# Order of a fused attention, gated convolution and feed-forward kernel: first loads and last block's steps rewritten

## The chip, the cores and the metric

One core of a Trainium2 chip (trn2) runs the kernel. The metric is the device time of one execution in microseconds; the median of the runs counts. The page and the trace come from one profiled execution. Engines: PE is TensorE, DVE VectorE, ACT ScalarE, POOL GpSimd, and SP is SyncE, whose queue issues all 360 DMA instructions of this kernel.

## What is computed

8 sequences of 576 tokens, 8 heads of 64 channels, all in float32. Attention runs in chunks of 64 tokens; its output, 512 channels, is gated by a causal convolution of five taps, and a normalized feed-forward part of 2048 hidden channels is added to it.

```python
scores = scale * np.matmul(q_c, k_c.transpose(0, 1, 2, 4, 3))      # per chunk of 64
attn = np.exp(scores - np.max(scores, axis=-1, keepdims=True))
attn = attn / (np.sum(attn, axis=-1, keepdims=True) + 1e-09)
x = np.matmul(attn, v_c)                                           # then (B, S, 512)
gate = 1.0 / (1.0 + np.exp(-sum(conv_w[k] * xp[:, k:k + S, :])))   # 5 taps, causal
x = gate * (x @ w_val) @ w_out
xn = (x - mu) / np.sqrt(var + 1e-06) * g_ln
out = x + np.maximum(xn @ w_ch1, 0.0) @ w_ch2
```

## The kernel before

The 4608 tokens are 18 units `u` of 256 tokens for the attention and 9 blocks `j` of 512 tokens for the gated part. Two units make a block. Products that need more than one pass of precision are split into a high and a low part, and three products are summed.

The steps of a unit: `sc(u)` (PE, 64 small matmuls of q and k), `mx` and `sub` (DVE, row maximum and difference), `exp` (ACT), `total` and `norm` (DVE, row sum, reciprocal and product), `turn` (PE, eight transposes), `turned` (ACT, copy to the tile pT), `pv` (PE, 64 small matmuls with v), `full`, `high`, `less`, `low` (ACT, ACT, PE, ACT: the result in full, its high part, the difference, its low part; tiles xf, xh, xl).

The steps of a block: `tap` and `taps` (ACT, DVE: the convolution), `sigm` (ACT), `val(j,f)` (PE, 12 matmuls), `gate`, `gate_high`, `gate_low` (DVE, ACT, DVE: product with the gate, its two parts gh and gl), `proj(j,t)` (PE, 12 matmuls over f = 0 to 3), `put(j,t)` (ACT copy and store). In block 0 two of the four channel groups run their convolution on PE: `conv_pe(f)`, ten matmuls, with `diag` and `sigm_pe` on ACT. `projp(j,t,f)` is a quarter of `proj`, three matmuls.

Weights arrive as pairs of 32-bit words and are unpacked: `w_copy` (ACT), `w_bits` (DVE, two instructions on the tile da), `w_high` (ACT), `w_low` (GpSimd). The prefix `ff_` marks the same steps for the first eight loads of the feed-forward weights, `ff_load(k)`, `ff_copy(k)` and so on. Block 0 of the feed-forward part is normalized beside block 8 of the gated part: `load_y0` (read of the stored block into yt0, 1 MB), `stats0`, `scale_a` to `scale_c`, `apply0`, `turn0`, `turned0`, `xn_high`, `xn_low`. Then come `ff1` and `ff2` of block 0, and the other eight blocks in four pairs.

What sets the order: up to the end of block 8's gated part, PE, DVE, ACT and SP follow a list of steps written out by hand, each engine in the order of that list (`tc.manual_schedule`). The first period (attention of units 0 to 5, block 0) is such a list; `period(j)` for j = 1 to 6 is a function that repeats; then blocks 7 and 8 are a list again. Behind it, only PE is ordered by hand.

The loads of the first period in this kernel: `load_qk(0)` to `load_qk(2)`, `load_v(0)` to `load_v(2)` and the four of `w_val` are issued ahead of the list (lines 759 to 770). `sc(u)` then issues `load_qk(u+2)`, `pv(u)` issues `load_v(u+3)`, and the step `load_o` issues the four loads of `w_out` together. A load of q and k is 1 MB, one of v or of a weight 0.5 MB. A load waits in SP's queue until its buffer is free (q and k have two buffers, v three), and what is queued behind it on SP waits too.

Of the kernel before, what the change touches and what calls it, by code (L numbers as in the profile page):

```python
# [10 lines left out]
U32 = mybir.dt.uint32  # L11
# [8 lines left out]
def tile_chunk_attention_gated_mlp(ctx: ExitStack, tc: tile.TileContext, qk, v, w_val, conv_w, w_out, g_ln, w1, w2, out):  # L20
# [143 lines left out]
    def sc(u):  # L164
        t = qkr.pop(u)
        kt, qt = t[:, 0], t[:, 1]
        ps = tsc[u] = ps_s.tile([P, 2, NG, CH], F32, tag="sc", name="sc")
        for g in range(NG):
            n, hp = divmod(g, NP)
            for c in range(2):  # L170
                cs = slice(n * P + c * CH, n * P + (c + 1) * CH)
                for par in range(2):
                    r0 = CH * par
                    nc.tensor.matmul(  # L174
                        out=ps[CH * c:CH * c + CH, par, g, :], lhsT=qt[r0:r0 + CH, hp, cs], rhs=kt[r0:r0 + CH, hp, cs],
                        start=True, stop=True,
                    )
        if 0 < u < NU - 2:
            load_qk(u + 2)

    def mx(u):
# [68 lines left out]
    def pv(u):  # L250
        t, va = tpT.pop(u), vr.pop(u)
        x = tx[u] = ps_x.tile([P, 2, NP // 2, UN], F32, tag="x", name="x")
        for i in range(NP // 2):
            for c in range(NC):
                n, cs = c // 2, slice(c % 2 * CH, (c % 2 + 1) * CH)
                for f in range(2):
                    for r in range(2):
                        r0, o0 = CH * r, CH * f
                        nc.tensor.matmul(  # L259
                            out=x[o0:o0 + CH, r, i, c * CH:(c + 1) * CH],  # L260
                            lhsT=va[r0:r0 + CH, c, 2 * i + f, :],
                            rhs=t[r0:r0 + CH, n * NP + 2 * i + f, cs],
                            start=(i == 0 and c == 0), stop=False, skip_group_check=True,
                        )
        if u + 3 < NU:
            load_v(u + 3)

    def part(t, u):
# [491 lines left out]
    cwu = stg.tile([KC * CT, P, 2], U32, tag="raw", name="cwu")  # L760
    nc.sync.dma_start(out=cwu.rearrange("r p w -> r (p w)"), in_=conv_w.rearrange("k (c p) w -> (k c) (p w)", p=P))
    nc.sync.dma_start(out=gr, in_=g_ln.rearrange("(c p) -> c p", p=P))
    load_w(w_val, "v", 0, 0, 1)
    load_qk(1)
    load_v(0)
    load_w(w_val, "v", 0, 1, 2)
    load_qk(2)
    load_v(1)
    load_w(w_val, "v", 0, 2, 4)
    load_v(2)  # L770

    s_0 = ExitStack()
    xn0, yt0, ps_t = None, None, None

# [122 lines left out]
        hs, ls = wv[nm + "s"]  # L897
        eng.tensor_tensor(out=ls[c], in0=fa.pop((nm, c)), in1=hs[c], op=ALU.subtract)

    def load_o():  # L900
        load_w(w_out, "o", CT)

    def diag(f):
        for i in range(KC):
# [79 lines left out]
        cnv(sigm, 3)  # L984

    with tc.manual_schedule(engines={mybir.EngineType.PE, mybir.EngineType.DVE, mybir.EngineType.Activation, mybir.EngineType.SP}):
        cwr_copy()
        sc(0)
        w_copy('v',0)
        cwr_bits()  # L990
        mx(0)
        sub(0)
        cw_turn()
        w_bits('v',0)
        exp(0)
        sc(1)
        w_copy('v',1)
        cw_copy()
        total(0)
        w_high('v',0)  # L1000
        mx(1)
        diag(0)
        sub(1)
        norm(0)
        sc(2)
        exp(1)
        w_copy('v',2)
        turn(0)
        mx(2)
        sub(2)  # L1010
        turned(0)
        exp(2)
        pv(0)
        w_low('v',0,nc.gpsimd)
        total(1)
        norm(1)
        turn(1,True)
        full(0)
        high(0)
        less(0)  # L1020
        total(2)
        turned(1)
        sc(3)
        low(0)
        norm(2)
        w_copy('v',3)
        mx(3)
        sub(3)
        pv(1)
        full(1)  # L1030
        load_o()
        turn(2,True)
        sc(4)
        w_bits('v',1)
        w_bits('v',3)
        high(1)
        w_high('v',1)
        w_low('v',1,nc.gpsimd)
        w_bits('v',2)
        mx(4)  # L1040
        diag(1)
        tap(0,3)
        less(1)
        sub(4)
        low(1)
        taps(0,3)
        turned(2)
        w_high('v',2)
        exp(3)
        w_copy('o',0)  # L1050
        conv_pe(0)
        w_bits('o',0)
        w_high('v',3)
        sc(5)
        total(3)
        exp(4)
        mx(5)
        pv(2)
        w_high('o',0)
        full(2)  # L1060
        high(2)
        norm(3)
        w_low('v',2,nc.gpsimd)
        conv_pe(1)
        w_copy('o',1)
        w_low('v',3,nc.gpsimd)
        less(2)
        val(0,0)
        tap(0,2)
        low(2)  # L1070
        w_copy('o',2)
        turn(3)
        taps(0,2)
        sigm_pe(0)
        sigm(0,3)
        w_bits('o',1)
        gate(0,0)
        total(4)
        w_low('o',0,nc.gpsimd)
        turned(3)  # L1080
        val(0,1)
        sigm_pe(1)
        pv(3)
        w_copy('o',3)
        val(0,2)
        w_bits('o',2)
        w_high('o',1)
        gate_high(0,0)
        sub(5)
        w_low('o',1,nc.gpsimd)  # L1090
        high(3)
        full(3)
        w_bits('o',3)
        norm(4)
        w_high('o',2)
        less(3)
        sigm(0,2)
        val(0,3)
        gate(0,1)
        gate_low(0,0)  # L1100
        low(3)
        gate(0,2)
        w_low('o',2,nc.gpsimd)
        turn(4)
        gate_high(0,1)
        w_high('o',3)
        gate_high(0,2)
        turned(4)
        gate_low(0,1)
        gate(0,3)  # L1110
        gate_low(0,2)
        gate_high(0,3)
        tap(1,2)
        pv(4)
        exp(5)
        tap(1,3)
        tap(1,0)
        w_low('o',3,nc.gpsimd)
        gate_low(0,3)
        full(4)  # L1120
        taps(1,2)
        taps(1,3)
        taps(1,0,1,2)
        proj(0,0)
        sigm(1,3)
        taps(1,0,2)
        proj(0,1)
        proj(0,2)
        proj(0,3)
        tap(1,1)  # L1130
        high(4)
        put(0,0)
        sigm(1,2)
        sigm(1,0)
        put(0,1)
        taps(1,1)
        sigm(1,1)
        put(0,2)
        less(4)
        low(4)  # L1140
        put(0,3)
        for j in range(1, NB - 2):
            period(j)
        norm(17)
        val(7,0)
        gate(7,0)
        val(7,1)
        ff_load(0)
        gate_high(7,0)
        gate(7,1)  # L1150
        val(7,2)
        ff_copy(0)
        ff_load(1)
        gate_high(7,1)
        gate_low(7,0)
        ff_bits(0)
        ff_load(2)
        gate(7,2)
        ff_copy(1)
        ff_high(0)  # L1160
        gate_low(7,1)
        ff_bits(1)
        turn(17)
        ff_low(0)
        gate_high(7,2)
        turned(17)
        gate_low(7,2)
        ff_copy(2)
        val(7,3)
        projp(7,0,0)  # L1170
        gate(7,3)
        pv(17)
        gate_high(7,3)
        projp(7,0,2)
        projp(7,0,1)
        full(17)
        ff_bits(2)
        projp(7,1,0)
        gate_low(7,3)
        tap(8,3)  # L1180
        tap(8,2)
        tap(8,0)
        projp(7,1,3)
        taps(8,3)
        ff_load(3)
        tap(8,1)
        projp(7,1,2)
        taps(8,2)
        projp(7,2,0)
        projp(7,2,1)  # L1190
        high(17)
        projp(7,0,3)
        projp(7,1,1)
        projp(7,3,0)
        taps(8,0,1,2)
        ff_high(1)
        ff_high(2)
        taps(8,1)
        projp(7,3,2)
        taps(8,0,2)  # L1200
        ff_low(2)
        projp(7,2,3)
        put(7,0)
        put(7,1)
        ff_low(1)
        ff_copy(3)
        projp(7,2,2)
        projp(7,3,3)
        projp(7,3,1)
        less(17)  # L1210
        sigm(8,2)
        sigm(8,3)
        put(7,2)
        put(7,3)
        low(17)
        prep()
        val(8,0)
        stats0(3)
        stats0(2)
        ff_load(4)  # L1220
        stats0(1)
        sigm(8,0)
        stats0(0)
        ff_copy(4)
        scale_a()
        sigm(8,1)
        val(8,1)
        gate(8,0)
        scale_b()
        val(8,2)  # L1230
        val(8,3)
        gate_high(8,0)
        gate(8,1)
        scale_c()
        gate_low(8,0)
        gate_high(8,1)
        apply0(2)
        apply0(0)
        apply0(1)
        gate_low(8,1)  # L1240
        gate(8,2)
        projp(8,0,0)
        turn0(0)
        gate(8,3)
        projp(8,1,0)
        gate_high(8,2)
        gate_low(8,2)
        turn0(1)
        apply0(3)
        gate_high(8,3)  # L1250
        turned0(0)
        gate_low(8,3)
        projp(8,0,1)
        projp(8,0,2)
        projp(8,1,1)
        projp(8,0,3)
        turned0(1)
        projp(8,1,3)
        ff_bits(3)
        ff_load(5)  # L1260
        turn0(2)
        xn_high(0)
        ff_bits(4)
        turn0(3)
        put(8,0)
        turned0(2)
        projp(8,1,2)
        projp(8,2,0)
        put(8,1)
        projp(8,2,2)  # L1270
        ff_copy(5)
        load_y0()
        projp(8,2,3)
        ff_load(6)
        projp(8,3,0)
        turned0(3)
        xn_high(2)
        xn_low(0)
        ff_bits(5)
        projp(8,2,1)  # L1280
        projp(8,3,1)
        ff_load(7)
# [135 lines left out]
```

## Time and profile before

| | us |
|---|---|
| runs of the kernel | 1071.51, 1072.88, 1073.88; median 1072.88 |
| profiled execution | 1072.09 |
| its span in the profile | 1070.3 |
| PE busy | 1041.0 (97%) |
| VectorE busy | 676.0 (63%) |
| ScalarE busy | 495.2 (46%) |
| GpSimd busy | 47.9 (4%) |
| moved by DMA | 155.26 MB |

All stretches below are microseconds from the start of the span. Busy time of an engine counts its instructions, without waits. The granted clock of PE (PEclk) is a share of its full 2.4 GHz, so 0.50 is its lower level of 1.2 GHz. "issue" as the end of a wait means that the trace shows nothing that the engine waited for.

### The profile page before, as it was taken

How to read it: one execution, taken by the hardware profiler on the slowest of the kernel's cores; microseconds unless marked ns; L12 is line 12 of the kernel's file. 1: busy time of each engine (PE TensorE's matmuls, PEld its weight loads, DVE VectorE, ACT ScalarE, POOL GpSimd, SP SyncE). 2: the span in 40 equal slices, each digit the busy share in tenths (PEclk: the TensorE clock that was granted, in tenths of full speed). 3: DMA queues.
4: the chain of work that ended last, by engine and by line, in shares of the span. 5: the costliest groups of instructions: out<-in, count | busy, mean ns of one | idle time of the engine just before them, and what ended most of it. 6: DMA issues, size and time to landing. Idle time of an engine off the chain costs nothing.

```text
span 1070.3 us, 16857 instructions
## 1 busy us (share of the span) xinstructions
PE 1041.0 (97%) x6778; PEld 855.3 (80%) x6778; DVE 676.0 (63%) x1112; ACT 495.2 (46%) x872; POOL 47.9 (4%) x74
## 2 busy tenths in 40 slices
PE   4899999999999999999999999999999999999998
PEld 4578888888778887888888888888888888888886
DVE  6899999998858896665465454258344438333434
ACT  4687766677767864444332234333233423222211
POOL 0210000000000003222100000000000000000000
PEclk9999999999999999999999999999999999999999
DMA  9614344413379836334427234325432324522202
GB/s 354 237 61 161 136 150 149 151 67 109 128 239 304 299 138 230 140 135 147 150 97 239 96 99 137 102 95 189 146 118 99 99 88 145 190 81 97 99 21 78
DMA packets 58580, 155.26 MB, mean 145 GB/s; under 512 B 5742, under 2 KB 13958, under 8 KB 56198
## 3 DMA queue, kind: packets, MB, share of 16 engines
q1 hardware_dynamic: 58502, 154.19, 41.6%
q8 instruction: 53, 0.87, 0.3%
q14 instruction: 25, 0.20, 0.1%
HBM read 116.41 MB, written 37.75 MB: 144 GB/s over the span
## 4 chain that ended last, share of the span: by engine, by line
PE 88%; DMA 5%; DVE 3%; ACT 2%; issue 1%; SPq 0%; ACTq 0%
PE psf L631 16%; PE acc L631 16%; PE x L663 16%; PE zy L663 12%; PE psv L346 8%; PE pso L346 7%; DMA raw<-in_moe_w_ch 3%; PE sc L174 2%; PE x L259 2%; PE acc L512 2%; PE pst L224 1%; DMA qkr<-in_qk 1%; PE pst L469 1%; PE pso L404 1%; PE psh L346 1%
## 5 line engine op out<-in xcount | busy, mean ns | idle before, releaser
L692 DVE TENSOR_TENSOR c<-x,c 128x512 f32<-128x512 f32 x96 | 66.2, 690 | 230.9 <-ACT c L687 183.2
L631 PE MATMUL psf<-w,h 128*128 128x512 f32 x768 | 187.6, 389 | 0.0
L631 PE MATMUL acc<-w,h 128*128 128x512 f32 x768 | 184.3, 389 | 0.0
L631 PEld LDWEIGHTS psf<-w,h 128*128 128x128 f32 x768 | 144.1, 188 | 30.3 <-DVE yt L636 0.4
L631 PEld LDWEIGHTS acc<-w,h 128*128 128x128 f32 x768 | 144.2, 188 | 29.9
L687 ACT ACTIVATE c<-zy 128x512 f32<-128x512 f32 x96 | 58.1, 606 | 203.3 <-PE zy L663 203.3
L663 PE MATMUL x<-t,wc 128*128 128x512 f32 x576 | 146.8, 390 | 0.8 <-DVE c L692 0.8
L663 PEld LDWEIGHTS x<-t,wc 128*128 128x128 f32 x576 | 107.7, 188 | 24.7 <-DVE c L692 2.1
L315 DVE SCALAR_TENSOR_TENSOR cg<-xf,cw,cg 128x516 f32<-128x516 f32 (+1 forms) x136 | 102.0, 766 | 4.4 <-ACT cg L307 1.0
L677 ACT ACTIVATE h<-c 128x512 fp32r<-128x512 f32 x96 | 60.5, 631 | 91.7 <-DVE c L692 46.9
L636 DVE TENSOR_TENSOR yt<-psf,yt 128x512 f32<-128x512 f32 x128 | 88.1, 689 | 21.0 <-PE psf L631 20.9
L663 PE MATMUL zy<-b,wc 128*128 128x512 f32 x384 | 98.6, 392 | 0.0
L663 PEld LDWEIGHTS zy<-b,wc 128*128 128x128 f32 x384 | 71.2, 188 | 14.2
L678 DVE SCALAR_TENSOR_TENSOR h<-c,h 128x512 fp32r<-128x512 f32 x96 | 69.0, 720 | 20.1 <-ACT h L677 18.6
L677 ACT ACTIVATE h<-x 128x512 fp32r<-128x512 f32 x32 | 19.1, 596 | 96.1 <-PE x L663 96.1
L346 PE MATMUL psv<-xh,vh 128*128 128x512 f32 x144 | 58.3, 405 | 1.2 <-ACT xl L301 1.2
L346 PE MATMUL psv<-xl,vh 128*128 128x512 f32 x144 | 56.2, 391 | 0.0
L346 PE MATMUL psv<-xh,vl 128*128 128x512 f32 x144 | 56.2, 391 | 0.0
L346 PE MATMUL psh<-xn,w 128*128 128x512 f32 x192 | 47.7, 398 | 2.1 <-DVE hl L497 2.1
L663 PE MATMUL x<-b,wc 128*128 128x512 f32 x192 | 48.9, 390 | 0.1
L663 PE MATMUL zy<-t,wc 128*128 128x512 f32 x192 | 48.7, 389 | 0.0
L346 PEld LDWEIGHTS psh<-xn,w 128*128 128x128 f32 x192 | 36.6, 191 | 10.7 <-DVE hl L497 2.5
(123 smaller groups left out, 1524.7 us busy)
## 6 DMA issues: line engine op xcount, KB each, us to landing
wc<-wc SPq DMA_DIRECT2D x112, 512.0 KB, 3.2
qkr<-in_qk SPq DMA_DIRECT2D x18, 1024.0 KB, 6.7
raw<-in_moe_w_ch SPq DMA_DIRECT2D x32, 512.0 KB, 5.6
vr<-in_v SPq DMA_DIRECT2D x18, 512.0 KB, 4.2
yd<-y SPq DMA_DIRECT2D x36, 256.0 KB, 2.2
out<-yt SPq DMA_DIRECT2D x36, 256.0 KB, 3.8
yr<-yd SPq DMA_DIRECT2D x32, 256.0 KB, 3.4
yt<-yd SPq DMA_DIRECT2D x32, 256.0 KB, 5.4
```

Of the source, the lines that this page charges most:

```text
L174: nc.tensor.matmul(out=ps[CH * c:CH * c + CH, par, g, :], lhsT=qt[r0:r0 + CH, hp, cs], rhs=kt[r0:r0 + CH, hp, cs], start=True, stop=True,)
L259: nc.tensor.matmul(out=x[o0:o0 + CH, r, i, c * CH:(c + 1) * CH], lhsT=va[r0:r0 + CH, c, 2 * i + f, :], rhs=t[r0:r0 + CH, n * NP + 2 * i + ...
L315: last_tap[j] = nc.vector.scalar_tensor_tensor(out=o, in0=xf[j][:, f, i:i + n], scalar=cw[:, i * CT + f:i * CT + f + 1], in1=o, op0=ALU.mu ...
L346: nc.tensor.matmul(out=ps, lhsT=lt, rhs=rh, start=(i == 0), stop=(i == n - 1))
L512: nc.tensor.matmul(out=acc[t], lhsT=lt, rhs=rh, start=(f == 0 and i == 0), stop=(f == NF - 1 and i == 2))
L631: nc.tensor.matmul(out=ps, lhsT=lt, rhs=rh, start=(g == 0 and k == 0 and (first or half)), stop=(g == 1 and k == 2 and (last or half)),)
L636: nc.vector.tensor_tensor(out=yt[i], in0=ps, in1=yt[i], op=ALU.add)
L663: nc.tensor.matmul(out=ps, lhsT=lt, rhs=rh, start=(start and c == 0 and i == 0), stop=(c == 1 and i == 2), skip_group_check=True)
L677: last_act = nc.scalar.activation(out=t[:, 0, :], in_=src, func=ACTF.Relu)
L678: last_relu = nc.vector.scalar_tensor_tensor(out=t[:, 1, :], in0=src, scalar=0.0, in1=t[:, 0, :], op0=ALU.max, op1=ALU.subtract)
L687: nc.scalar.activation(out=t, in_=zy, func=ACTF.Copy)
L692: nc.vector.tensor_tensor(out=t, in0=x, in1=t, op=ALU.add)
```

## The change

The operations, their number and their sizes are the same in both kernels, on each engine; the low parts of the attention weights (`w_low`) run on GpSimd in both. What changes is order.

1. The loads of the first period become steps of the list, each at a place of its own, `load_o` is cut into four, and a bound keeps `sc` and `pv` from issuing these loads themselves.
2. The list of the first period has another order.
3. The list of blocks 7 and 8 has another order. `load_y0` is issued twice in both kernels, in `prep()` and near the end of block 8; the second of these moves.

```diff
+    AHEAD = 5
-        if 0 < u < NU - 2:
+        if AHEAD < u < NU - 2:
             load_qk(u + 2)
-        if u + 3 < NU:
+        if AHEAD - 1 < u < NU - 3:
             load_v(u + 3)
-    load_qk(0)
...
-    load_w(w_val, "v", 0, 2, 4)
-    load_v(2)
-    def load_o():
-        load_w(w_out, "o", CT)
+    def load_wv(c):
+        load_w(w_val, "v", 0, c, c + 1)
+
+    def load_wo(c):
+        load_w(w_out, "o", CT, c, c + 1)
     with tc.manual_schedule(engines={mybir.EngineType.PE, mybir.EngineType.DVE, mybir.EngineType.Activation, mybir.EngineType.SP}):
+        load_qk(0)
+        load_cw()
+        sc(0)
         cwr_copy()
-        sc(0)
...
```

On PE, the first steps of the first period before, from sc(1) on (rows of L174 are sc, L224 turn, L259 pv, L295 less, L336 conv_pe):

```order
L174 MATMUL sc_227<-qkr_161 64x64 x32
L174 MATMUL sc_291<-qkr_167 64x64 x32
L224 MATMUL pst_329<-ident_140,pr_289 128x128 x8
L259 MATMUL x_345<-pT_341,vr_163 64x64 x32
L224 MATMUL pst_386<-ident_140,pr_384 128x128 x4
L224 MATMUL pst_387<-ident_140,pr_384 128x128 x4
L295 MATMUL x_345<-xh_398,neg_142 128x512 x2
L174 MATMUL sc_409<-qkr_260 64x64 x32
L259 MATMUL x_453<-pT_406,vr_169 64x64 x32
```

The same steps now (lines are one higher):

```order
L175 MATMUL sc_225<-qkr_206 64x64 x32
L225 MATMUL pst_263<-ident_140,pr_220 128x128 x8
L260 MATMUL x_297<-pT_294,vr_260 64x64 x32
L175 MATMUL sc_330<-qkr_272 64x64 x32
L296 MATMUL x_297<-xh_375,neg_142 128x512 x2
L225 MATMUL pst_388<-ident_140,pr_371 128x128 x4
L225 MATMUL pst_389<-ident_140,pr_371 128x128 x4
L260 MATMUL x_408<-pT_400,vr_378 64x64 x32
L175 MATMUL sc_443<-qkr_441 64x64 x32
```

sc(2) stood ahead of turn(0) and pv(0) and stands behind them; pv(1) stood behind sc(3) and stands ahead of it.

On SP, the loads from qk(1) to qk(4) before (qkr is a load of q and k, vr one of v, raw one of a weight):

```order
L80 DMA qkr_161<-in_qk 128x2048
L84 DMA vr_163<-in_v 128x1024
L114 DMA raw_165<-in_moe_w_val 128x1024
L80 DMA qkr_167<-in_qk 128x2048
L84 DMA vr_169<-in_v 128x1024
L114 DMA raw_171<-in_moe_w_val 128x1024
L114 DMA raw_173<-in_moe_w_val 128x1024
L84 DMA vr_175<-in_v 128x1024
L80 DMA qkr_260<-in_qk 128x2048
L80 DMA qkr_324<-in_qk 128x2048
```

The same stretch now:

```order
L81 DMA qkr_206<-in_qk 128x2048
L115 DMA raw_213<-in_moe_w_val 128x1024
L115 DMA raw_222<-in_moe_w_val 128x1024
L85 DMA vr_260<-in_v 128x1024
L81 DMA qkr_272<-in_qk 128x2048
L115 DMA raw_292<-in_moe_w_val 128x1024
L115 DMA raw_366<-in_moe_w_out 128x1024
L85 DMA vr_378<-in_v 128x1024
L81 DMA qkr_441<-in_qk 128x2048
L85 DMA vr_484<-in_v 128x1024
L115 DMA raw_487<-in_moe_w_out 128x1024
L81 DMA qkr_492<-in_qk 128x2048
```

One value weight moved ahead of qk(2), and the output weights are spread among the loads of the units instead of standing together further back.

On SP, the end of block 8 before (raw1 are feed-forward weights, yd8 stores of block 8, yt0 the read of block 0 by load_y0, and the last two rows the next feed-forward weights):

```order
L834 DMA raw1_3609<-in_moe2_w_ch2 128x1024
L848 DMA ad2_89<-da_3485 128x512
L410 DMA yd8_139<-y_3625 128x512
L410 DMA yd8_139<-y_3639 128x512
L791 DMA yt0_3454<-yd0_131 128x4x512
L836 DMA raw1_3651<-in_moe2_w_ch1 128x4x256
L834 DMA raw1_3671<-in_moe2_w_ch2 128x1024
L410 DMA yd8_139<-y_3675 128x512
L410 DMA yd8_139<-y_3687 128x512
L848 DMA ad3_90<-da_3692 128x512
L130 DMA raw1_3730<-in_moe2_w_ch1 128x4x256
```

The same stretch now:

```order
L822 DMA raw1_3561<-in_moe2_w_ch2 128x1024
L836 DMA ad2_89<-da_3555 128x512
L824 DMA raw1_3611<-in_moe2_w_ch1 128x4x256
L411 DMA yd8_139<-y_3629 128x512
L411 DMA yd8_139<-y_3641 128x512
L822 DMA raw1_3662<-in_moe2_w_ch2 128x1024
L411 DMA yd8_139<-y_3677 128x512
L836 DMA ad3_90<-da_3682 128x512
L411 DMA yd8_139<-y_3693 128x512
L779 DMA yt0_3446<-yd0_131 128x4x512
L131 DMA raw1_3730<-in_moe2_w_ch1 128x4x256
```

The load of ff_load(6), raw1_3651 and now raw1_3611, stood behind two stores and load_y0 and stands ahead of them; load_y0 is now the last step ahead of the weights of the feed-forward part.

## Rows read from the trace of the kernel before

**Rows 1.** The page's first part: engine, busy us, share, instructions.

```profile
PE 1041.0 (97%) x6778; PEld 855.3 (80%) x6778; DVE 676.0 (63%) x1112; ACT 495.2 (46%) x872; POOL 47.9 (4%) x74
```

**Rows 2.** Table of windows: busy us of each engine, clock, DMA share, GB/s.

```profile
10.00:70.00 60.00, 46.96 (x769) 35.29 (x770) 51.31 (x63) 43.77 (x67) 12.44 (x11) 0.94 0.61 234
70.00:240.00 170.00, 170.00 (x2144) 140.21 (x2144) 156.64 (x222) 122.80 (x168) 1.75 (x11) 1.00 0.37 131
240.00:320.00 80.00, 76.24 (x458) 61.82 (x458) 61.39 (x105) 53.79 (x93) 0.00 (x0) 0.98 0.47 154
320.00:380.00 60.00, 59.64 (x278) 49.14 (x277) 51.60 (x125) 45.95 (x100) 0.00 (x0) 1.00 0.90 303
380.00:1070.00 690.00, 685.86 (x3068) 566.73 (x3066) 352.35 (x597) 226.66 (x445) 32.87 (x42) 1.00 0.36 124
```

**Rows 3.** Timeline of TensorE: start, us, instructions, idle time before and its releaser.

```profile
16.31 1.99 PE L174 MATMUL sc<-qkr 64*64 64x64 f32 x64 [3.82 <-DMA qkr<-in_qk]
...
21.31 1.16 PE L259 MATMUL x<-pT,vr 64*64 64x64 f32 x64 [1.11 <-ACT pT L233]
23.58 1.69 PE L224 MATMUL pst<-ident,pr 128*128 128x128 f32 x8 [1.11 <-DVE pr L211]
```

**Rows 4.** The chain of waits from 0 to 85 us: start, us, what.

```profile
32.27 4.29 PE psc L336 x10
...
39.02 4.08 issue
...
43.55 6.19 PE psc L336 x10
...
64.75 1.03 ACT pT L233
...
78.59 2.72 PE psv L346 x12
```

**Rows 5.** DMA queues from 31 to 38 us: packets, MB, share of the engines.

```profile
q1 hardware_dynamic: 736, 2.91, 101.3%
```

**Rows 6.** DMA queues from 38 to 43.2 us.

```profile
q1 hardware_dynamic: 318, 2.16, 99.7%
q8 instruction: 1, 0.02, 1.2%
```

**Rows 7.** The page's DMA queues, of the whole span.

```profile
q8 instruction: 53, 0.87, 0.3%
```

**Rows 8.** Table of windows at two places where the clock is low.

```profile
45.00:47.00 2.00, 2.00 (x3) 0.67 (x2) 1.61 (x4) 1.76 (x3) 0.00 (x0) 0.50 0.59 227
...
314.00:317.00 3.00, 3.00 (x9) 2.33 (x8) 1.40 (x3) 0.68 (x2) 0.00 (x0) 0.51 0.81 224
```

**Rows 9.** Timeline of VectorE in the first period.

```profile
12.75 1.21 DVE L184 TENSOR_REDUCE mx<-sc 128x16 f32<-128x1024 f32 x1
...
15.41 1.22 DVE L211 TENSOR_TENSOR pr<-ex,sm 128x1024 f32<-128x1024 f32 x1
...
31.31 0.42 DVE L91 TENSOR_SCALAR da<-da 128x512 uint32<-128x512 uint32 x1
...
32.38 1.49 DVE L91 TENSOR_SCALAR da<-da 128x512 uint32<-128x512 uint32 x1
...
66.94 12.25 DVE L315 SCALAR_TENSOR_TENSOR cg<-xf,cw,cg 128x516 f32<-128x516 f32 x16
```

**Rows 10.** Waits from 270 to 330 us: engine, line, releaser, us, times, longest.

```profile
PE psh L346 <- DVE hl L497: 2.1, 1, 2.1
...
PE psv L346 <- ACT xl L301: 1.2, 1, 1.2
```

**Rows 11.** Timelines of ScalarE and of SP in the last block.

```profile
310.13 0.66 ACT L87 ACTIVATE da<-raw 128x512 f32<-128x512 f32 x1 [3.98 <-DMA raw<-in_moe_w_ch]
...
300.84 0.41 SPq L791 DMA_DIRECT2D yt<-yd  x1
301.34 0.52 SPq L836 DMA_DIRECT2D raw<-in_moe_w_ch  x1
```

More of the change, by code (lines that the diff above doesn't have):

```diff
@@ L1069, in tile_chunk_attention_gated_mlp @@
[L1069 to L1075, printed above, removed]
-        w_bits('o',1)
-        gate(0,0)
+        w_copy('o',2)
+        exp(4)
+        pv(2)
+        load_v(3)
+        sigm_pe(0)
+        full(2)
+        w_low('o',0,nc.gpsimd)
+        sigm(0,2)
+        val(0,0)
+        w_bits('o',2)
+        high(2)
+        val(0,1)
+        taps(0,3)
+        gate(0,0)
+        gate_high(0,0)
+        w_copy('o',3)
+        sigm_pe(1)
@@ L1078, in tile_chunk_attention_gated_mlp @@
+        sigm(0,3)
+        load_v(4)
+        less(2)
+        low(2)
+        val(0,2)
+        total(3)
+        norm(3)
+        turn(3)
+        sc(5)
+        load_v(5)
+        gate_low(0,0)
+        w_bits('o',1)
+        w_high('o',1)
+        w_high('o',2)
+        turned(3)
+        gate(0,1)
+        gate_high(0,1)
+        load_qk(6)
+        w_bits('o',3)
         total(4)
[L1079 to L1082, printed above, removed]
+        gate(0,2)
+        w_high('o',3)
@@ L1152, in tile_chunk_attention_gated_mlp @@
         ff_copy(0)
+        turned(17)
+        pv(17)
         ff_load(1)
+        gate_low(7,0)
+        val(7,3)
+        ff_bits(0)
+        ff_high(0)
+        ff_load(2)
+        ff_copy(1)
+        projp(7,0,0)
         gate_high(7,1)
-        gate_low(7,0)
-        ff_bits(0)
-        ff_load(2)
+        full(17)
         gate(7,2)
-        ff_copy(1)
-        ff_high(0)
+        ff_low(0)
+        ff_bits(1)
         gate_low(7,1)
-        ff_bits(1)
-        turn(17)
-        ff_low(0)
@@ L1165, in tile_chunk_attention_gated_mlp @@
         gate_high(7,2)
-        turned(17)
         gate_low(7,2)
-        ff_copy(2)
-        val(7,3)
-        projp(7,0,0)
+        projp(7,1,0)
+        projp(7,2,0)
         gate(7,3)
-        pv(17)
-        gate_high(7,3)
+        tap(8,0)
         projp(7,0,2)
[L1175 to L1180, printed above, removed]
-        tap(8,2)
[L1182 to L1186, printed above, removed]
@@ new lines, in tile_chunk_attention_gated_mlp @@
+        less(17)
+        tap(8,3)
+        ff_high(1)
+        taps(8,2)
+        projp(7,1,1)
+        gate_high(7,3)
+        gate_low(7,3)
+        ff_copy(2)
+        taps(8,0,1,2)
+        projp(7,3,2)
+        low(17)
+        projp(7,0,3)
+        projp(7,0,1)
+        taps(8,3)
+        projp(7,1,2)
+        projp(7,1,3)
+        ff_copy(3)
+        put(7,0)
+        projp(7,2,2)
+        taps(8,0,2)
+        tap(8,1)
+        put(7,1)
+        projp(7,2,3)
+        put(7,2)
+        sigm(8,3)
@@ L1232, in tile_chunk_attention_gated_mlp @@
+        ff_bits(2)
+        sigm(8,1)
         gate_high(8,0)
         gate(8,1)
-        scale_c()
+        ff_high(2)
         gate_low(8,0)
         gate_high(8,1)
+        stats0(0)
+        stats0(3)
+        stats0(1)
+        stats0(2)
+        sigm(8,2)
+        val(8,2)
+        scale_a()
+        val(8,3)
+        ff_high(3)
+        gate(8,2)
+        scale_b()
+        ff_load(4)
+        gate_high(8,2)
+        scale_c()
+        ff_copy(4)
+        apply0(0)
+        gate_low(8,1)
```

335 lines of the change are left out of this document (149 added, 186 removed).

## The prediction

> **What bounds the kernel now.** I read the page's first part and then a table of windows. TensorE is busy for 1041.0 of 1070.3 us [rows 1], so no more than 29 us of idle time can be won; the change removes no instruction (both kernels issue the same operations on every engine). The windows say where the idle time lies [rows 2]: 13.0 us in 10 to 70, nothing in 70 to 240, 3.8 in 240 to 320, 0.4 in 320 to 380, and 4.1 in the 690 us behind. The first 10 us hold the rest, and in them sc(0) waits for the very first load, which the change leaves where it is. Two stretches are therefore open to this change, and they are the two that it rewrites. Between them TensorE is full, so whatever is won before 70 us is carried to 240 as long as no other engine takes over as the bound; VectorE, busy for 156.64 of those 170 us, is the one that could.
>
> I then read TensorE's timeline and the chain of waits for 0 to 85 us, to see what ends each gap [rows 3, 4]. sc(2) stands for 3.82 us behind the load of qk(2); pv(0) waits 1.11 for the copy pT; turn(1) waits 1.11 for norm(1); pv(2) breaks off after 51 of its 64 matmuls and stands for 4.08 us with no releaser; pv(4) waits for pT again, whose copy takes 1.03 [rows 4]. There is a cost that is not idle time as well: behind the 4.08 the granted clock reads 0.50, the lower level of 1.2 GHz [rows 8], and conv_pe(1) takes 6.19 us where conv_pe(0), the same ten matmuls at the full level, takes 4.29 [rows 4].
>
> The 4.08 needs a reading of its own. The matmuls of pv(2) wait for nothing that the trace shows. From 31 to 38 us the load queue fills the DMA engines alone, at 101.3%, and the only instruction packet of 38 to 43.2 comes through in that second window [rows 5, 6]. The instruction queue moved 53 packets in 0.87 MB, 16 KB each [rows 7]; TensorE's 6778 matmuls and 6778 weight loads, divided by 53, make 256 a packet. Up to where pv(2) breaks off, the written order has issued 603 matmuls, 1206 instructions. So I read the gap as a packet of instructions that came late behind the loads. That is an inference.
>
> **The first period, part by part.** The span ends 1.8 us before the profiled run's own time (1072.09), and the sum is made against that run.
> - Loads. Their number, sizes and queue stay. Ahead of qk(2) now stand three value-weight loads and v(0), where two and v(0) stood: 0.5 MB more, 1.2 us at the 2.91 MB in 7 us of [rows 5]. qk(2) then lands near 17.4.
> - sc(2) moves behind turn(0) and pv(0). TensorE is free at 12.5 (16.31 less 3.82). turn(0) needs norm(0), which today ends at 16.6, and stands now ahead of mx(1) and sub(1), which take from 12.75 to 15.2 [rows 9]: it ends near 14.2. So the wait of 3.82 shrinks to about 1.8, **2.0 won**. pv(0)'s 1.11 for pT stays. sc(2) comes at 18.6, later than its load: with that the load costs nothing, up to 1.2 us of further delay.
> - sc(2)'s 2 us stand now between pv(0) and turn(1), and cover the 1.11 for norm(1): **1.1 won**.
> - The packet gap. In the new order the 603rd matmul falls in turn(3), behind three chains of val(0,·); I place it near 49 us, when the twelve loads behind qk(2), up to v(4), have been through (7.5 MB, some 18 us from 17.4 at the same rate). Most likely the gap is gone: **4.1 won**, and the 6.19 becomes 4.29: **1.9 won**. Its bounds are below.
> - turn(4) and pv(4) get proj(0,1) between them, twelve matmuls against a copy of 1.03: **1.0 won**.
> - New waits. conv_pe(1) now takes its PSUM buffer behind turned(2), a copy of the kind that pT's 1.03 us shows [rows 4], with only sc(4) between: 0 to 1.0, I take 0.8. proj(0,0) stands right behind val(0,3) and needs gl(0,3) for its last matmuls, behind gate(0,3), mx(5) and gate_low(0,3) on VectorE: 0 to 2, I take **1.0**.
> - GpSimd's low parts. They run on GpSimd in both kernels, in another place. Beside one, a bits step of VectorE reads 1.49 us in place of 0.42 [rows 9]; that stretch exists today and only changes its victim, 0.
>
> Sum: 2.0 + 1.1 + 4.1 + 1.9 + 1.0 less 1.8 gives **8.3 us**, and val(1,0), now at 78.59, would start near 70.3. VectorE must come along: its sixteen taps of block 1 end today at 79.2 [rows 9], 0.6 behind. From 10 to 70 it is busy for 51.31 of 60 [rows 2], from 70 to 79.2 with nothing but these taps, so it can come earlier by its idle 8.7 us at the most: the taps end at 70.5 at the best, and with 1 to 3 us of idle kept at 71.5 to 73.5, 1 to 3 behind TensorE. It regains 13 us in the 170 behind, some 3 a period, so I charge nothing, and keep 3 us as this term's bound.
>
> **The last block.** The waits of 270 to 330 name two on TensorE that matter: val(8,0) 1.2 for xl(17), and ff1(2) 2.1 for the split of ff1(0)'s result [rows 10]. The second starts on ScalarE: its queue stands 3.98 us at ff_copy(6), whose load was issued at 301.34 behind load_y0 at 300.84 [rows 11], and the copies of ff1's result stand behind it. After that wait the clock falls to 0.51 for 3 us [rows 8], 1.5 us lost. The new order puts less(17), high(17) and low(17) before the last projections of block 7, which gives val(8,0) its 1.2; it issues ff_load(6) ahead of put(8,0), and load_y0 only behind put(8,3), so ff_copy(6) finds its data. Won: 1.2 + 2.1 + 1.5 = 4.8. Against that, turn0 and projp(8,·) are now interleaved more closely, and each turn0 waits for an apply0: 0 to 2, I take 0.8. **4.0 us.** What could swallow it: in 320 to 380 the DMA engines are 90% busy [rows 2]; the weight loads of the feed-forward part stand behind the moved load_y0. But they are issued behind ff_bits(6), which comes earlier too, and TensorE idles for only 0.4 us there.
>
> The 690 us behind have an unchanged order on TensorE with 4.1 us of gaps [rows 2], 0.
>
> **Sum.** 1072.09 - 8.3 - 4.0 = 1059.8 for the profiled run. The median of the runs shown, 1072.88, lies 0.8 higher, so against it the forecast is 1060.6.
>
> **A rule against this.** In that 5.2 us window the load queue has 99.7 of the engines' time and the instruction queue 1.2, one packet [rows 6]. The Trainium skill, "DMA: Bandwidth & Descriptors", section "Queues, rings and completion order", says that each DMA engine goes round between the queue rows that have work, one packet at a time. By that rule an instruction packet would pass a full load queue almost at once, the 4.08 would not be a fetch, and reordering loads would not remove it: the sum would be the first rival's. The gap, in the one window with a full queue and a packet boundary, speaks against it, though the trace does not show when the packet was asked for.
>
> **The rivals.**
> 1. One gap with the loads stays. A packet boundary now falls every 128 matmuls: at the start of sc(3), near 25 us, and in sc(4), near 33, both while the queue is still full. If one of them waits as pv(2) did, 4.1 and the 1.9 of clock come back: 1066.6. For it: loads run to about 35 us in the new order too. Against it: the clock and gap of today appear at one of the four or five boundaries in 10 to 50 us.
> 2. VectorE becomes the bound. If its lag of up to 3 us is handed on in period 1, the first term falls to 5.3: 1063.6. For it: 92% busy in 70 to 240. Against it: it regains some 3 us a period.
> 3. The loads of the feed-forward part set the pace in 320 to 380, and the 4.0 is lost there: 1064.6. For it: DMA share 0.90. Against it: the loads start earlier as well.
> 4. Slower. Rival 1's mechanism at more places: each late packet costs 4.1 + 1.9 = 6.0. Two late ones give 1072.6, no change; from the third on (sc(3), sc(4) and turn(3) all caught) the kernel is slower, 1078.6.
> 5. The change does little of what it says: the low parts on GpSimd are there already, so that part is worth 0 in every case above.
>
> **How the numbers follow.** A measurement of this kernel can tell about 0.2%, 2.1 us, from no change. Forecast 0.52; rival 1 0.13; rival 2 0.12; rival 3 0.11; two late packets, or several of the partial losses together, 0.07; three late packets 0.05. So faster 0.88, same 0.07, slower 0.05. Low end: all of the new waits at 0 and the full 4.8: 1060.6 - 1.8 - 0.8 = 1058.0, and some 2.5 us of short gaps that I left in place (pv(0)'s 1.1, and those in 28 to 38): 1055. High end: each of rivals 1 to 3 alone, with 1.4 us for the unknown waits at their upper bounds: 1068.
>
> **What would show it.** Right: turn(0) near 14.3 and before sc(2); no gap over 2 us on TensorE between 20 and 50; ten matmuls of conv_pe(1) in 4.3 us; val(1,0) near 70.3; no wait of ff1(2) for hl, and a clock of 1.00 from 300 to 320. Wrong: gaps with no releaser inside sc(3) or sc(4), and lower clock behind them (rival 1); val of block 1 waiting for VectorE (rival 2); TensorE waiting for weights behind 320 (rival 3).

## The result: 1.3% faster, and the profile after

The changed kernel took 1059.63 us (median of four runs, 1059.17 to 1060.81), the kernel before 1073.38 beside it; the ratio is 0.9872, 95% interval 0.985 to 0.9894. The forecast was 1060.6 in a range of 1055 to 1068. On a second chip, beside more runs of before, it took 1059.17 against 1071.70, ratio 0.9886 (0.9827 to 0.9945).

The profiled execution of the changed kernel took 1060.81 us, its span is 1059.0: 11.3 us less than the profiled one of before. Its busy times show the same work on each engine (busy us, share, instructions); TensorE's 4.1 us less than in [rows 1] are for the most part the clock, as below:

```profile
PE 1036.9 (98%) x6778; PEld 852.6 (81%) x6778; DVE 675.9 (64%) x1112; ACT 494.3 (47%) x872; POOL 47.4 (4%) x74
```

The table of windows of the changed kernel, cut where its own stages end, answers to [rows 2]:

```profile
10.00:70.00 60.00, 51.83 (x800) 39.42 (x801) 57.43 (x70) 47.37 (x74) 11.86 (x11) 1.00 0.60 230
70.00:240.00 170.00, 169.89 (x2148) 140.16 (x2147) 157.39 (x224) 123.98 (x169) 1.74 (x11) 1.00 0.38 133
240.00:310.00 70.00, 69.30 (x433) 56.42 (x432) 55.18 (x97) 49.26 (x86) 0.00 (x0) 1.00 0.51 174
310.00:370.00 60.00, 59.00 (x277) 49.01 (x276) 52.38 (x127) 46.17 (x101) 0.00 (x0) 1.00 0.88 299
370.00:1059.00 689.00, 684.58 (x3061) 565.52 (x3060) 351.11 (x595) 225.29 (x443) 32.94 (x42) 1.00 0.37 124
```

In 10 to 70 us TensorE idles for 8.2 us in place of 13.0, and the granted clock is at its full level throughout, where it was 0.94 on average. In the last two blocks it idles for 0.7 in place of 3.8. What is left in the first 60 us stands in the waits of TensorE from 0 to 130 us (us in total, times, longest):

```profile
PE sc L175 <- DMA qkr<-in_qk: 6.2, 1, 6.2
PE pst L225 <- DVE pr L212: 2.7, 1, 2.7
PE sc L175 <- DVE ex L191: 2.3, 1, 2.3
PE x L260 <- ACT pT L234: 2.1, 3, 1.1
PE x L296 <- ACT xh L289: 1.2, 2, 0.6
PE x L296 <- ACT xf L284: 0.7, 1, 0.7
PE psc L337 <- ACT pT L234: 0.4, 1, 0.4
```

The wait for qk(2) and the gap with no releaser are gone. Behind the first load, what remains are waits for VectorE and ScalarE, the longest of 2.7 us. TensorE's timeline shows the steps in their new places, val(1,0) last:

```profile
15.51 1.97 PE L225 MATMUL pst<-ident,pr 128*128 128x128 f32 x8 [2.72 <-DVE pr L212]
...
22.64 0.73 PE L296 MATMUL x<-xh,neg 128*128 128x512 f32 x2 [0.64 <-ACT xh L289]
23.21 1.03 PE L225 MATMUL pst<-ident,pr 128*128 128x128 f32 x8
24.97 1.42 PE L260 MATMUL x<-pT,vr 64*64 64x64 f32 x64 [0.73 <-ACT pT L234]
...
34.94 4.56 PE L337 MATMUL psc<-xf,dg 128*128 128x512 f32 x10 [0.35 <-ACT pT L234]
...
71.52 0.39 PE L347 MATMUL psv<-xh,vh 128*128 128x512 f32 x1
```

val(1,0) starts at 71.52, and before at 78.42 in the same view. The rest is read at the first matmul of ff2 of block 0. This is its row in the view of the tile acc, for the changed kernel (durations, then the first and the last start):

```profile
L513 PE MATMUL acc<-w,hh x128: 389/389/477, 305.4 to 395.4; 128*128 128x512 f32 x128
```

It started at 316.7 before, so it comes 11.3 us earlier; the last matmul of the kernel moved from 1066.4 to 1055.1, 11.3 us as well. Between, the first proj of block 1 moved from 94.22 to 87.49. So the first period gave 6.7 to 6.9 us, the last two blocks 4.6, and behind them nothing was won or lost in sum.

### The profile page after: what moved, and what is told of

Its sections match the earlier page's. It is cut to its first block, busy times and chain, and to the rows that moved or that the text cites. A ratio compares the mean times of both kernels' runs of the same rounds, so it can differ in the third digit from the quotient of the medians.

```text
span 1059.0 us, 16853 instructions
## 1 busy us (share of the span) xinstructions
PE 1036.9 (98%) x6778; PEld 852.6 (81%) x6778; DVE 675.9 (64%) x1112; ACT 494.3 (47%) x872; POOL 47.4 (4%) x74
## 4 chain that ended last, share of the span: by engine, by line
PE 88%; DVE 6%; ACT 2%; DMA 2%; issue 1%; SPq 0%; ACTq 0%; DVEq 0%
PE psf L632 16%; PE acc L632 16%; PE x L664 16%; PE zy L664 12%; PE psv L347 7%; PE pso L347 6%; PE psh L347 3%; PE acc L513 2%; PE pso L405 2%; DVE cg L316 2%; PE x L260 2%; PE pst L470 1%; PE sc L175 1%; PE pst L225 1%; DMA raw<-in_moe_w_ch 1%; PE x L296 1%
## 5 line engine op out<-in xcount | busy, mean ns | idle before, releaser
L347 PE MATMUL pso<-oh,gh 128*128 128x512 f32 x112 | 45.0, 402 | 0.0
```

Source lines behind the costliest of these rows:

```text
L347: nc.tensor.matmul(out=ps, lhsT=lt, rhs=rh, start=(i == 0), stop=(i == n - 1))
```

## The experiments

Twelve runs were made on three occasions, each beside runs of the kernel before. Times are medians in us; val(1,0), ff2 (of block 0) and the last matmul are starts in the profiled execution. A dash stands where the profiled execution is the only one (e3, e8, e10), so that there is no interval.

| run | us | before beside it | ratio, 95% interval | val(1,0) | ff2 | last matmul |
|---|---|---|---|---|---|---|
| before (profile ahead) | | | | 78.42 | 316.7 | 1066.4 |
| changed | 1059.63 | 1073.38 | 0.9872 (0.985 to 0.9894) | 71.52 | 305.4 | 1055.1 |
| e1, first period alone | 1065.93 | 1070.51 | 0.9956 (0.9938 to 0.9974) | 71.72 | 308.8 | 1059.4 |
| e2, last blocks alone | 1064.61 | 1070.51 | 0.9943 (0.9921 to 0.9965) | 78.11 | 311.9 | 1060.4 |
| e3, qk(6), qk(7) later | 1070.27 | 1070.51 | - | 73.34 | 310.2 | 1064.5 |
| e4, and weights later | 1068.75 | 1070.51 | 0.9994 (0.997 to 1.0017) | 73.48 | 310.7 | 1065.7 |
| e5, load_y0 later | 1064.95 | 1071.70 | 0.9942 (0.9915 to 0.9969) | 78.72 | 313.4 | 1063.0 |
| e6, new steps, old load places | 1065.15 | 1071.70 | 0.9947 (0.9924 to 0.9969) | 76.93 | 310.9 | 1059.3 |
| e7, low parts on VectorE | 1062.47 | 1071.70 | 0.9917 (0.9892 to 0.9941) | 74.27 | 308.1 | 1056.5 |
| a2, changed again | 1059.17 | 1071.70 | 0.9886 (0.9827 to 0.9945) | 71.59 | 305.4 | 1053.8 |
| e8, changed, full queue | 1064.40 | 1072.02 | - | 76.13 | 310.0 | 1058.4 |
| e9, changed, first load split | 1059.35 | 1072.02 | 0.9887 (0.9854 to 0.9921) | 71.74 | 305.7 | 1053.8 |
| e10, before, weights later | 1071.03 | 1072.02 | - | 77.97 | 313.7 | 1065.3 |
| e11, e1 and load_y0 later | 1061.16 | 1072.02 | 0.9901 (0.9861 to 0.994) | 71.12 | 306.5 | 1055.2 |

### The two halves of the change, and whether they add

e1 is the changed kernel with the list of blocks 7 and 8 as it was before; e2 is the kernel before with only that list replaced; a2 is the changed kernel once more.

```diff
 # e1, against the changed kernel (e2 is the reverse, against the kernel before)
         for j in range(1, NB - 2):
             period(j)
+        norm(17)
         val(7,0)
-        norm(17)
         gate(7,0)
...
```

> The new first period with its loads, and the last block in the order of before. Theory: the two parts add, and TensorE full between them carries the first one through: val of block 1 about 7 us earlier than before, and the end too, so a ratio of 0.992 to 0.994. Rival (the load chain of the feed-forward part sets the pace, so that an earlier start alone is given back): within 0.2% of before.

> The first period of before, and the new order of the last two blocks alone. Theory: ff2 of block 0 starts about 4.6 us earlier than before and the end comes 4 to 5 us earlier, ratio 0.995 to 0.997; no wait of ff1(2) for the split, no low clock at 314 us. Rival (the loads behind 320 us swallow it): the end moves by less than 2 us.

> The changed kernel itself, on the chip of these runs: 12 to 14 us below the kernel before, and the sum of what the first period alone (4.7 us in its runs) and the last block alone (6.1 us) gave, if the two parts only add; several us more than that sum if they help each other.

Each half alone makes the kernel faster: 0.9956 and 0.9943. Their product is 0.9899, the whole gave 0.9886 and 0.9872: within the intervals they add. In the profiles e1 keeps the 6.7 us of val(1,0) to the last matmul (1066.4 to 1059.4, 7.0); its median shows less, 4.6, and its ratio misses the 0.992 to 0.994 that was expected. e2 moves ff2 by 4.8 and the last matmul by 6.0.

### Of the last blocks, the place of one load

e5 is the kernel before with one line moved; e11 has the new first period and the old list of blocks 7 and 8 with that line moved.

```diff
         ff_copy(5)
-        load_y0()
         projp(8,2,3)
         ff_load(6)
...
         put(8,3)
+        load_y0()
```

> The kernel before, with the second load_y0 alone moved behind put(8,3), so that ff_load(6) no longer stands behind its 1 MB. Theory (that load is what ScalarE's queue, and behind it ff1(2), waits for): ff_copy(6) waits under 2 us in place of 4, ff1(2) waits under 0.5 us in place of 2.1, the clock stays full at 314 us, ff2 of block 0 starts 3 to 3.6 us earlier and the end comes 2 to 3.6 us earlier, ratio about 0.997. Rival (the other reordering of the last block does it): ff2 moves by less than 1 us.

> The new first period, and the last block in the order of before with only the second load_y0 moved behind put(8,3). Theory (of the last block's new order, the place of load_y0 is what counts): within 2.5 us of the changed kernel, 1.2 of them the wait of val(8,0) that stays. Rival (the rest of the new order counts as much): 3 to 5 us above the changed kernel.

In e5, ff_copy(6) on ScalarE starts with no wait, and the copy of ff1's result follows less than 3 us behind it; before, the same copy stood 3.98 us, until 310.13 [rows 11]. ScalarE's timeline in e5:

```profile
306.30 0.68 ACT L87 ACTIVATE da<-raw 128x512 f32<-128x512 f32 x1
...
308.74 0.58 ACT L496 ACTIVATE hh<-psh 128x512 fp32r<-128x512 f32 x1
```

ff1(2)'s wait is gone from TensorE's waits, ff2 starts 3.3 us earlier, and the last matmul comes 3.4 earlier, with the first period as slow as before. The medians gave more, 6.8 us, and a ratio of 0.9942 where about 0.997 was expected: the profiled execution, 1068.72, was the slowest of e5's ten, which begin at 1062.52. e11 comes within 2.0 us of the changed kernel, and its one large wait in the last blocks is the 1.2 of val(8,0) that stays, as the waits of TensorE in e11 from 270 to 330 us show:

```profile
PE psv L347 <- ACT xl L302: 1.2, 1, 1.2
PE pst L470 <- ACT yt L453: 0.5, 1, 0.5
```

So in the profiles 3.3 of the 4.6 us of the last blocks are the place of load_y0, and 1.2 are the wait of val(8,0), which goes when less(17) and low(17) stand ahead of the last projections; the other exchanges there do little. By the medians the share of load_y0 is larger, and how large is open.

### Steps or places of the loads

e6 is the changed kernel with the loads of the first period where they were before: qk(0) to qk(2), the value weights and v(0) to v(2) ahead, the others issued by sc and pv, and the four output weights together behind full(1).

```diff
-    AHEAD = 5
+    AHEAD = 0
...
         full(1)
+        load_wo(0)
+        load_wo(1)
+        load_wo(2)
+        load_wo(3)
```

> The changed kernel with every load of the first period in the place that it had before (issued ahead, by sc and pv, and the four output weights together); the steps of all engines in the new order. Theory (the order of the steps does it, since no packet boundary and no wait for a load falls where TensorE needs it): val(1,0) at 71 to 73, the end within 2 us of the changed kernel. Rival (the places of the loads do it): a gap of TensorE with no releaser or a wait for a load of over 2 us comes back, and val(1,0) is later than 74.

The theory was wrong, and the rival came by its second way, a wait for a load: val(1,0) falls back to 76.93, and 6.0 us of the median are lost. ScalarE and TensorE in e6:

```profile
35.10 0.66 ACT L88 ACTIVATE da<-raw 128x512 f32<-128x512 f32 x1 [5.80 <-DMA raw<-in_moe_w_out]
```

```profile
40.19 6.40 PE L337 MATMUL psc<-xf,dg 128*128 128x512 f32 x10 [6.97 <-ACT pT L234]
```

The new list has w_copy('o',0) earlier on ScalarE, ahead of turned(2). With the output weights issued late, ScalarE stands at that copy for 5.80 us, turned(2) behind it, and conv_pe(1) waits 6.97; behind that idle time the ten matmuls run slower once more (6.40 against 4.56). So the new order of steps, without the new places of the loads, gives the whole kernel no more than the last blocks alone gave (0.9947 against e2's 0.9943): the copies need their loads earlier too. The new places with the old steps were not tried; e3, e4 and e10 only hold some loads back. No gap without a releaser came back, so for that the new order of steps was enough.

### The gap in pv(2)

e3, e4 and e10 are the kernel before with loads taken out of the queue ahead of pv(2).

```diff
-        if 0 < u < NU - 2:
+        if 0 < u < NU - 2 and u not in (4, 5):
             load_qk(u + 2)
...
         pv(2)
+        load_o(1, CT)
+        load_qk(6)
+        load_qk(7)
```

This is e4. e3 has the two load_qk lines and leaves load_o whole, in its place; e10 has load_o cut in two as here, and leaves the loads of q and k in theirs.

> The kernel before, with the loads of qk(6) and qk(7) issued only behind pv(2): 2 MB less in the queue while TensorE works towards pv(2); the four output weights stay there. Theory (an instruction packet waits behind the queue): the gap of 4.08 us in pv(2) shrinks to 1 to 3 us, since the queue empties some 2.4 us earlier. Rival (the gap is no fetch and has to do with none of the loads): still 4.1 us at the same matmul.

> The kernel before, with qk(6), qk(7) and three of the four output weights issued only behind pv(2): the queue is empty near 36 us. Theory: no gap in pv(2), conv_pe(1) at the full clock in 4.3 us, val(0,0) near 44 to 46 in place of 50.2; what of these 6 us reaches val(1,0), now at 78.59, is 2 to 6 us, since VectorE stands close behind there. Rival (no fetch): the gap of 4.1 us stays.

> The kernel before, with three of the four output weights issued only behind pv(2), and qk(6) and qk(7) in their places. Theory (the packet waits for the loads queued ahead): a queue that ends 3.6 us earlier, near 39, and a gap in pv(2) of 0 to 2 us. Rival (the moment of the packet has other causes): a gap of 3 to 4 us as before.

The timeline of TensorE at pv(2), first in e2, whose first period is that of before, then in e4, e10 and e3:

```profile
38.10 0.98 PE L259 MATMUL x<-pT,vr 64*64 64x64 f32 x51
42.89 0.70 PE L259 MATMUL x<-pT,vr 64*64 64x64 f32 x13 [3.81 <-issue]
```

```profile
36.63 0.98 PE L259 MATMUL x<-pT,vr 64*64 64x64 f32 x51
39.23 0.45 PE L259 MATMUL x<-pT,vr 64*64 64x64 f32 x13 [1.62 <-issue]
```

```profile
37.85 0.98 PE L259 MATMUL x<-pT,vr 64*64 64x64 f32 x51
40.17 0.45 PE L259 MATMUL x<-pT,vr 64*64 64x64 f32 x13 [1.34 <-issue]
```

```profile
37.12 1.14 PE L259 MATMUL x<-pT,vr 64*64 64x64 f32 x64
```

The stop comes behind the same 51st matmul each time, whatever the time (in e5, which has the first period of before, as well, for 3.81 us). That fits the end of a packet of instructions and nothing that depends on data. In e4 the DMA engines move nothing at all from 34.5 to 36.5 us; then one packet comes, the row of the queues from 36.5 to 37, and TensorE goes on at 39.23:

```profile
q8 instruction: 1, 0.02, 14.8%
```

The time of the packet parts the gap in two. With an empty or nearly empty queue it moves 1.1 us behind the start of sc(5): at 36.74 in e4, where sc(5) starts at 35.68, and at 37.95 in e10 (36.90). With a full queue it moves 3.5 to 3.7 us behind it: at 40.77 in the kernel before, 40.68 in e2, 41.28 in e5 (37.09, 37.15 and 37.70). In all five TensorE goes on 2.2 to 2.5 us after the packet begins to move. So 1.3 to 1.6 us of the stop are there with an idle queue, and some 2.5 come with a full one; when the packet was asked for, no trace shows. In e3 there is no gap: its packet came already at 33.5 to 34.5, while the queue was full (97.1% of the engines' time). Why that one was early, the runs do not show. e3 and e10 are one execution each; the expectation of e10 came, those of e3 (1 to 3 us) and e4 (no gap) missed to either side.

A shorter stop is not yet a gain. In e10 the stop and the clock behind it are 4.4 us cheaper, and val(1,0) comes only 0.45 earlier: of the held-back weights ScalarE waits 2.13 us for one, and pv(4) waits 2.22 for pT, with the low clock behind it.

A late packet in a full queue was then made on purpose. e8 is the changed kernel with four copies of w_val, 2 MB each, to memory that no step reads (`busy_loads`):

```diff
         load_v(4)
+        busy_loads()
         less(2)
```

> The changed kernel with four copies of 2 MB between places of the chip's memory, which nothing reads, issued behind load_v(4): the queue stays full from 28 us to past 50. Theory (an instruction packet is served behind the loads queued before it): the packet that TensorE needs in turn(3), at 50 us, comes late, a gap with no releaser of 1 to 5 us appears there or in the next 128 matmuls, and val(1,0) starts later than 73. Rival (the queues are served in turn): packets come within 3 us as in the changed kernel, no gap, val(1,0) at 71 to 73.

TensorE in e8, at pv(3), and the window 50 to 60 us:

```profile
52.40 1.14 PE L260 MATMUL x<-pT,vr 64*64 64x64 f32 x58 [0.26 <-ACT pT L234]
56.19 0.49 PE L260 MATMUL x<-pT,vr 64*64 64x64 f32 x6 [2.65 <-issue]
```

```profile
50.00:60.00 10.00, 7.09 (x145) 5.84 (x144) 7.44 (x10) 6.51 (x9) 4.43 (x4) 0.77 0.98 318
```

The changed kernel has no stop in pv(3); the packet ahead of it moves at 49.94 us there, and at 53.76 in e8. With the queue full there is a stop of 2.65 us behind the 58th matmul, the low clock follows it, and val(1,0) comes 4.5 us later than in a2, the last matmul 4.6. Up to this stop the written order has issued 730 matmuls, 127 more than the 603 ahead of the stop in pv(2): with their weight loads that is 254 instructions, where a packet holds 256. That is the best sign that the two stops are of one kind.

The stop came as the theory said, but not by the theory's queue. The four copies were issued by 33.1 us, and 2 MB of them moved after the instruction packet, so it did not wait for everything queued ahead. The copies move in pieces of 64 KB, 3.3 us each, as the row of the queues of e8 from 49 to 53.5 us has it (pieces, MB, share of the engines' time):

```profile
q1 hardware_dynamic: 16, 1.05, 73.4%
```

The instruction packet came 3.8 us later than in the changed kernel, little more than one such piece. The Trainium skill ("DMA: Bandwidth & Descriptors", "Queues, rings and completion order") has each DMA engine go round between the queues, and drain a whole packet of one before it turns to the next. That allows a wait for what is being moved and excludes one for the whole queue, and e8 agrees; so this rule does not speak against a late packet, as the prediction had it. In the kernel before, a piece of a load takes 0.26 us (318 in 5.2 us of 16 engines, [rows 6]), and the packet was some 2.5 us late. What it waited for there is open.

### What a gain of the first period is worth behind 320 us

e3 and e4 had their val(1,0) 5.1 and 4.9 us earlier, and their ff2 6.5 and 6.0 earlier, but the last matmul only 1.9 and 0.7. The timeline of TensorE in e3 from 320 to 375 us has these waits:

```profile
331.03 0.73 PE L346 MATMUL psh<-xn,w 128*128 128x512 f32 x2 [0.71 <-ACT w L99]
331.99 2.56 PE L346 MATMUL psh<-xn,w 128*128 128x512 f32 x10 [0.22 <-DVE w L100]
366.57 0.66 PE L469 MATMUL pst<-ident,yr 128*128 128x128 f32 x4 [2.54 <-ACT xt L474]
```

The copies and splits of the feed-forward weights and ScalarE's copy xt are late there. ScalarE itself stands in e3 for 8.7 us from 318 to 372 us until loads of these weights land, as the third rival said, and in the old list of the last blocks that gives back most of the gain. Both are one profiled execution, and that of e4 (1071.47) was 2.7 above its median; its median gains 1.8 us, which its interval does not tell from nothing. e1, with the same list, gave back less (1.00 us at the same place), and the changed kernel 1.00, where 0.35 stood before. In a2, the second profile of the changed kernel, nothing stands there.

### The low parts, and the first load

e7 puts the eight low parts of the attention block's weights on VectorE (the first two lines below are one of the eight); e9 cuts the first load in two by heads (the other lines), and sc(0) goes through the first half first.

```diff
-        w_low('v',0,nc.gpsimd)
+        w_low('v',0,nc.vector)
...
+        if u == 0:
+            for a in (0, NP // 2):
+                nc.sync.dma_start(out=t[:, :, a:a + NP // 2], in_=src[:, :, a:a + NP // 2])
```

> The changed kernel with the eight low parts of the attention block's weights on VectorE in place of GpSimd. Theory (VectorE runs without a pause from 20 to 74 us and sets the start of period 1): its eight subtractions of 0.68 us add 5.4 us, and the stretched steps beside GpSimd (some 4 us) fall away, so val(1,0) and the end come 0.5 to 3 us later. Rival (TensorE sets the pace there): within 0.5 us of the changed kernel.

> The changed kernel with the first load, qk(0), cut into two halves by heads and sc(0) going through the first half first. Theory (the first microseconds are a chain from that load through sc(0), VectorE and ScalarE): sc(0) starts 1 to 2 us earlier and ends 0.5 to 1 us earlier, and the end comes 0.5 to 1 us earlier. Rival (smaller pieces of memory make the load slower): sc(0) ends no earlier, or up to 1 us later.

e7 is 3.3 us slower than a2 beside it, val(1,0) 2.7 later. VectorE has hardly more to do: it is busy for 58.98 us from 10 us to val(1,0), and for 58.65 in a2, so the eight subtractions cost about what the stretched steps give back. The loss is in the order. In e7 a weight copy on ScalarE stands 2.01 us for one of the low parts, turned(2) stands behind it, and conv_pe(1) waits 2.15 for pT in place of 0.34, the path of e6; proj(0,0) waits 1.17 for another low part. The product of norm(0) in the changed kernel, the GpSimd instruction that runs beside it, and the same product in e7:

```profile
13.45 2.00 DVE L212 TENSOR_TENSOR pr<-ex,sm 128x1024 f32<-128x1024 f32 x1
```

```profile
13.11 1.27 POOL L886 TENSOR_TENSOR vl<-da,vh 128x512 fp32r<-128x512 f32 x1 [11.67 <-ACT vh L882]
```

```profile
13.01 1.22 DVE L212 TENSOR_TENSOR pr<-ex,sm 128x1024 f32<-128x1024 f32 x1
```

2.00 us beside GpSimd, 1.22 without. The Trainium skill ("SBUF — State Buffer", "SBUF: two separate sides") says that VectorE, in an operation with two inputs there, and GpSimd share one pair of ports, and that whichever starts first has it for its whole instruction. By that the product would stand from 13.45 to GpSimd's end at 14.38, an estimate of 0.93 us; the 0.78 agrees to 0.15. In e9 the product starts first, at 14.49, and takes 1.23; GpSimd's 1.27 then becomes 2.16 in the profile.

e9's timeline of TensorE shows both halves of sc(0):

```profile
5.28 1.13 PE L180 MATMUL sc<-qkr 64*64 64x64 f32 x32 [5.28 <-DMA qkr<-in_qk]
8.06 1.13 PE L180 MATMUL sc<-qkr 64*64 64x64 f32 x32 [1.65 <-DMA qkr<-in_qk]
```

The first half starts only 0.4 us earlier than the whole in a2 (5.72), and the second 2.3 later than that: two halves were slower than the whole, as the rival had it. The end did not move (1059.35 against 1059.17): of the 1.5 us by which sc(0) ended later (the rival had up to 1), 0.6 were left at turn(0), since norm(0)'s product was not stretched this time, and 0.15 at val(1,0).

## Why the prediction was right, step by step

- **turn(0) ahead of sc(2), 2.0 us.** Right in kind, 1.1 in size. turn(0) waits 2.72 for norm(0), not 1.8. I had priced GpSimd's low parts at 0, as a stretch that only changes its victim; the new victim is norm(0)'s product, on which TensorE waits, and it costs 0.8. In e7, where it is not stretched, turn(0) waits 1.88.
- **sc(2) over the wait for norm(1), 1.1 us.** That wait is gone, but less(0) and pv(1) now wait 0.64 and 0.73 for ScalarE's copies. Worth nothing net.
- **The gap and the clock behind it, 4.1 and 1.9 us.** Both came: no gap without a releaser, conv_pe(1) in 4.56 where that view had 6.26, and 1.00 for the granted clock. The reason was half right. A late packet of instructions fits every run (the same matmul in the old order, one packet further on in e8), but the loads are only some 2.5 us of the 4.1; 1.3 to 1.6 stay with an empty queue (e4, e10). It is not the whole queue that holds the packet up, as e8 shows. Nor did before have only one packet in a full queue: another moved at 24.7 us, with 92% of the engines' time taken by loads, and TensorE did not stop.
- **How safe the new order is.** By the count of matmuls its packets of 36.7 and 49.9 us are needed near 50 and 53.6. With the 2.2 to 2.5 us between a packet and its use, the second has little over 1 us to spare. That no packet was late (rival 1) is in part luck.
- **pv(4) behind proj(0,1), 1.0 us.** Right; pv(4) has no wait.
- **New waits, 1.8 us.** Right in sum, wrong in place. proj(0,0) never waited for gl(0,3) (I had 1.0), conv_pe(1) waits 0.35 (I had 0.8), and I missed 0.58, 0.29 and 0.65 at less(2), pv(3) and less(3).
- **Left out.** Ahead of sc(4) and sc(5) TensorE stood 0.70 and 0.52 us before, with no releaser. I had left these short gaps in place; they are gone, 1.2 us that make up for more than half of what the first two terms lack. That is luck.
- **Sum of the first period.** 8.3 forecast, 6.9 measured at val(1,0). The windows give 4.9 of it as idle time; the other 2.0 are TensorE's shorter busy time, the clock. The terms that were mis-sized are the first two: 1.1 and 0 in place of 2.0 and 1.1.
- **VectorE.** The taps of block 1 end at 73.3 (forecast 71.5 to 73.5), and in 70 to 240 TensorE idled for 0.11 us, so rival 2 did not come. The 3 us that VectorE was to regain in a period are 2.3: 13.4 us in 170, at 29.35 us a period. e7 shows how near VectorE and ScalarE are: with almost the same busy time on VectorE, in another order, 3.3 us are lost.
- **The last two blocks, 4.0 us.** 4.6, by the mechanism that was named: load_y0 ahead of ff_load(6) (3.3 of them, e5) and val(8,0)'s wait (1.2, e11).
- **The loads behind 320 us.** 0.65 us were lost there in one profile (1.00 against 0.35) and none in the other (a2), inside the range. e3 and e4 show the third rival with the old list: there 3 to 4 of 5 us were gone at the end.
- **The places of the loads.** I priced them at nothing, since their cover was sc(2)'s new place. e6 says that without them the new order loses 5.3 us at val(1,0) against a2, by a wait on ScalarE that I had not looked for: w_copy('o',0) had moved ahead of turned(2).
- **The range.** At their upper bounds the new waits of the first period are 1.2 above what I took (3.0 less 1.8), and turn0's another 1.2; the high end has 1.4 for both. The result is far from that end.
- **Sum.** 12.3 forecast; 11.3 between the two profiled executions, 13.7 and 12.5 between the medians. The first period's 1.4 too much and the last blocks' 0.6 too little partly cancel, and both lie within what two occasions differ by.

## What to carry to other kernels

Where one queue carries all loads, the place of a load in the written order is part of the order of every engine that unpacks it: moving a copy forward on an engine that keeps its order, without its load, can cost most of the gain (5.3 of 6.9 us here), and one large read ahead of a small urgent one is a wait somewhere else. A gain early in a long chain is only worth what the next stage with a busy queue lets through, so read that stage's slack, its shortest wait included, before adding the gain up. A stretch beside another engine is priced by the instruction that it falls on, and not by its sum. And one profile is one execution: where runs of a kernel differ by 10 us, ask which of them it shows.

## What the runs showed of the hardware

- TensorE can stop at a fixed place in the program, behind a packet of instructions that comes late: 1.3 to 1.6 us with DMA engines that are idle (e4, e10), 3.8 to 4.1 with a full load queue (before, e2, e5), 2.65 one packet further on when the queue was filled on purpose (e8). It goes on 2.2 to 2.5 us after the packet begins to move, in all six.
- Whichever of VectorE's product and GpSimd's subtraction started first kept its time (1.23 and 1.27 us); the other was stretched (2.00 in the changed kernel, 2.16 on GpSimd in e9).
- Cutting a 1 MB load into two by heads made the whole land later: its second half was used 2.3 us after the time at which the uncut load was ready (e9).
- The kernel before spread over 1066.5 to 1076.7 us in its runs, the changed one over 1058.4 to 1060.8. The low clock goes with it: of the 55 runs of before that stand beside the experiments, the four with a mean granted clock of 1.000 took 1066.9 to 1068.6 us, the fourteen with 0.995 or less 1071.3 to 1076.7. So the stretches of low clock are not in every execution; the profiled one, at 0.995, has them. Whether the gap and the load chain ahead of them are missing in the quicker ones was not seen, as none of those was profiled.
